# K and V in rows of 64 KiB, V blocks in turn in one overlapping buffer

One core of one Trainium2 chip. The metric is the device time of one execution in microseconds (us), median of several executions. Profiled spans are some 2 us shorter than the timed executions.

## The reference, cut to what matters

One decode step of an attention layer over a long cache, times a small gated dense branch:

```python
q = xn @ wq                                   # 1 x (16 heads x 256)
scores = einsum("bhqd,bhkd->bhqk", q, k_cache) * 256 ** -0.5   # 65536 keys per head
o = einsum("bhqk,bhkd->bhqd", softmax(scores), v_cache)
s = o.reshape(1, 1, 4096) @ wo
out = x + s * silu(silu(xn @ w1) @ w2)        # xn = layernorm(x), x: 1 x 1 x 448
```

K and V are 16 x 65536 x 256 bf16 each, 1074 MB together, and each byte is used once. The weights are 10.6 MB.

## The kernel before

A block is 128 partitions x 128 keys (4 blocks per head, 64 in all). Each block of K, and of V, comes as two tiles of 64 keys, 32 KiB per partition, each into its own buffer. VectorE multiplies K by the query (19 of 32 keys with a fused multiply and sum, 13 as one product that ScalarE then sums), ScalarE makes the exponentials, TensorE multiplies them with V, two keys per matmul. Scores of block i run beside V of block i - 1.

```python
KT, SUB, ND, TPB = 64, 32, 19, 2
Kt = [pool.tile([P, KT * Dh], bf16, name=f"K{t}") for t in range(TPB)]
Vt = [pool.tile([P, KT * Dh], bf16, name=f"V{t}") for t in range(TPB)]

def sp_block(i):                      # the only issuer of the stream
    for t in range(TPB):
        take(sp, kf[t])               # K buffer t is free
        sp.dma_start(out=Kt[t][:, :], in_=src(Kd, i, t)).then_inc(kl[t], 16)
        take(sp, vf[t])               # V buffer t is free
        sp.dma_start(out=Vt[t][:, :], in_=src(Vd, i - 1, t)).then_inc(vl[t], 16)

def pe_attend():
    take(pe, pv)                      # exponentials of the block
    for t in range(TPB):
        take(pe, vl[t], 16)           # V tile t has landed
        pe_keys(psO, Vt[t], 0, t * KT, KT, t == 0, t == TPB - 1, ...)   # 32 matmuls, then the buffer is free
# ... query copied per block from a broadcast table; products go to separate buffers prod[], junk_d[], junk_a[]
# ... start (layernorm, q, dense branch), last block and output projection left out
```

## Time and profile before

| | before |
|---|---|
| median, range of 4 | 2529.24 us, 2528.04 to 2529.59 |
| DMA, mid-run | 16 engines busy, 432 GB/s |
| one block (16 MiB of K and V), mid-run | 38.87 us |
| VectorE, TensorE, ScalarE busy | 88%, 51%, 57% |
| last packet of the stream, end | 2519.7, 2527.2 us |

A DMA of 128 rows is spread over 16 DMA engines, 8 rows each, one packet per row here. The engines do not march together: one ends its share up to 4 us before another. "Landing" below is the end of the slowest engine's share; a block's period is the time from one landing of V to the next; a burst is the run of matmuls that multiplies one block's exponentials with V; the release is the moment in a burst after which the next V may be issued, and its lead is the time from that issue to the moment when the first engine has done its share of the K queued before it. Packet times are from the trace's records of single packets, put on the same clock as the instructions; they do not name the engine, so what is said of single engines is put together from the times. The lines themselves are in the prediction.

### The profile page before, as it was taken

The numbers are of one execution on the slowest core, as the hardware profiler recorded it, in microseconds if no ns is written. First come the engines' busy times: TensorE is split into PE (matmuls) and PEld (weight loads), VectorE is DVE, ScalarE is ACT, GpSimd is POOL, SyncE is SP. The second block draws the span as 40 slices with busy tenths as digits, with TensorE's granted clock in tenths as the row PEclk, the third lists the DMA queues.
The fourth block names the chain that finished last, engine by engine and source line by source line (L and its number), as shares of the span: only waits on it lengthen the run. The fifth ranks groups of instructions, "written<-read, shape, count | busy, mean of one in ns | idle before, by whom it ended". The sixth has DMA issues, their size and how long they took to land. (4 is left out here: it accounts for less than half of the span.)

```text
span 2527.2 us, 30558 instructions
## 1 busy us (share of the span) xinstructions
PE 1284.5 (51%) x4945; PEld 483.4 (19%) x4945; DVE 2219.2 (88%) x10276; ACT 1446.6 (57%) x6996; POOL 1.4 (0%) x12
## 2 busy tenths in 40 slices
PE   3554455455544554555455445544554455445547
PEld 1111121111111211111112111111121111111212
DVE  7989898898898988988989889889898898898886
ACT  5656565655565656555656565556565655565553
POOL 0000000000000000000000000000000000000000
PEclk7777777777777777777767776777677767776778
DMA  9999999999999999999999999999999999999998
GB/s 413 432 432 432 432 432 432 432 432 432 432 432 433 432 433 432 432 432 432 432 432 432 432 432 432 432 432 432 432 432 432 432 432 433 432 432 432 432 432 346
DMA packets 40450, 1084.46 MB, mean 429 GB/s; under 512 B 4338, under 2 KB 6516, under 8 KB 6644
## 3 DMA queue, kind: packets, MB, share of 16 engines
q1 hardware_dynamic: 40434, 1084.31, 99.8%
q8 instruction: 4, 0.07, 0.0%
q14 instruction: 10, 0.08, 0.0%
q10 hardware_dynamic: 2, 0.00, 0.0%
HBM read 1084.29 MB, written 0.00 MB: 429 GB/s over the span
## 5 line engine op out<-in xcount | busy, mean ns | idle before, releaser
L262 ACT ACTIVATE junk_a<-prod 128x256 bf16<-128x256 bf16 x3328 | 1330.7, 401 | 746.9 <-ACTq L141 746.9
L308 PE MATMUL psO<-V,PV 128*2 128x512 bf16 x4064 | 1165.2, 458 | 1097.6 <-PEq L141 1097.6
L226 DVE CUSTOM_DVE_ANT_0 junk_d<-K,qcur 128x256 bf16<-128x256 bf16 x4864 | 1698.7, 414 | 0.0
L308 PEld LDWEIGHTS psO<-V,PV 128*2 128x2 bf16 x4064 | 388.4, 97 | 1847.6 <-issue 1520.3
L212 DVE TENSOR_TENSOR prod<-K,qcur 128x3328 bf16<-128x3328 bf16 x256 | 482.9, 1886 | 247.0 <-DVEq L141 247.0
L262 ACT ACTIVATION_READ_ACCUMULATOR junk_a<-prod 128x1 f32 x3328 | 620.0, 186 | 0.0
L226 DVE DVE_READ_ACCUMULATOR2_ANT S<- 128x1 f32 x4864 | 374.2, 77 | 0.0
L295 ACT COPY O<-psO 2x512 f32<-2x512 f32 x64 | 36.8, 574 | 202.4 <-ACTq L141 202.4
L343 PE MATMUL ps_t<-eye,O 2*128 2x1 f32 x520 | 69.6, 251 | 48.4 <-PEq L141 48.4
L343 PEld LDWEIGHTS ps_t<-eye,O 2*128 2x128 f32 x520 | 65.9, 192 | 69.0 <-issue 68.9
L297 ACT COPY hist<-ps_t 128x2 f32 (+1 forms) x65 | 10.4, 160 | 94.9 <-ACTq L141 94.9
L301 PE MATMUL ps_nb<-gmax,ones_row 1*128 1x1 bf16 x65 | 10.3, 159 | 56.1 <-PEq L141 55.6
L191 DVE COPY qcur<-qb 128x256 bf16 (+1 forms) x64 | 14.5, 227 | 25.4 <-issue 15.8
L284 ACT ACTIVATE PV<-S,hist 128x128 bf16<-128x128 f32 (+1 forms) x65 | 26.0, 400 | 2.1
L199 DVE COPY S<-S 128x128 f32<-128x128 f32 (+1 forms) x65 | 14.7, 226 | 9.5
L200 DVE TENSOR_REDUCE rmax<-S 128x1 bf16<-128x128 f32 (+1 forms) x65 | 18.2, 280 | 0.2 <-issue 0.2
L180 DVE TENSOR_REDUCE gmax<-ps_m 1x1 bf16<-1x128 f32 x65 | 17.8, 274 | 0.5 <-DVEq L141 0.5
L301 PEld LDWEIGHTS ps_nb<-gmax,ones_row 1*128 1x128 bf16 x65 | 6.0, 92 | 60.8 <-issue 60.5
L333 PE MATMUL ps_m<-ident,rmax 128*1 128x128 bf16 x65 | 14.3, 220 | 5.7 <-PEq L141 5.7
L488 PE MATMUL ps_a<-xnT,V 128*64 128x1 bf16 x112 | 6.7, 256 | 18.2 <-DMA V<-in_B_w_dram 18.2
L284 ACT ACTIVATION_READ_ACCUMULATOR PV<-S,hist (+1 forms) x65 | 12.1, 186 | 0.0
L488 PEld LDWEIGHTS ps_a<-xnT,V 128*64 128x64 bf16 x112 | 6.6, 210 | 18.7 <-DMA V<-in_B_w_dram 18.7
(65 smaller groups left out, 79.3 us busy)
## 6 DMA issues: line engine op xcount, KB each, us to landing
K<-in_A_k_cache_dram SPq DMA_DIRECT2D x126, 4096.0 KB, 21.3
V<-in_A_v_cache_dram SPq DMA_DIRECT2D x125, 4096.0 KB, 28.7
K<-in_A_k_cache_dram SPq DMA_DIRECT2D x4, 2048.0 KB, 18.5
V<-in_A_v_cache_dram SPq DMA_DIRECT2D x4, 2048.0 KB, 22.9
W<-in_A_v_cache_dram SPq DMA_DIRECT2D x2, 2048.0 KB, 27.3
W<-in_A_wq_dram SPq DMA_DIRECT2D x1, 3072.0 KB, 10.4
K<-in_A_wo_dram SPq DMA_DIRECT2D x3, 896.0 KB, 31.4
V<-in_B_w_dram SPq DMA_DIRECT2D x1, 1568.0 KB, 35.5
```

Source lines behind the costliest of these rows:

```text
L180: dve.reduce_max(out=gmax[0:1, :], in_=ps_m[0:1, :], axis=AX.X).then_inc(gm, 1)
L191: q_t = own(dve.tensor_copy(out=qcur[:, :], in_=qb[:, sub(q0, Dh)]))
L199: dve.tensor_copy(out=S2[:, c0:c1], in_=S[:, c0:c1]).then_inc(f, 1)
L200: dve.reduce_max(out=rmax[:, :], in_=S[:, c0:c1], axis=AX.X).then_inc(rm, 1)
L212: m = dve.tensor_tensor(out=prod[k % 2][:, :, :], in0=Kv[:, s * SUB + ND : (s + 1) * SUB, :], in1=qcur[:, None, :].to_broadcast([P, NA, Dh ...
L226: ins = dve.tensor_tensor_reduce(out=junk_d[jk][:, :], in0=Kv[:, s * SUB + j, :], in1=qcur[:, :], scale=1.0, scalar=0.0, op0=ALU.mult, op1 ...
L262: ins = act.activation(out=junk_a[jk][:, :], in_=prod[k % 2][:, j, :], func=ACT.Identity, accum_out=S[:, a : a + 1],)
L284: act.activation(out=PV[:, c0:c1], in_=S2[:, c0:c1], func=ACT.Exp, bias=neg, scale=scale, accum_out=hist[:, at(i), 1:2].rearrange("p o s - ...
L295: act.copy(out=O[:, :], in_=po[:, :]).then_inc(oc, 1)
L301: pe.matmul(ps_nb[:, 0:1], lhsT=ones_row[0:1, :], rhs=gmax[0:1, :], start=True, stop=True).then_inc(bm, 1)
L308: ins = pe.matmul(po[:, :], lhsT=PV[:, c0 + c : c0 + c + 2], rhs=T[:, (k0 + c) * Dh : (k0 + c + 2) * Dh], start=(start and c == 0), stop=( ...
L343: ins = pe.matmul(ps_t[:, a : a + 1], lhsT=Ov[:, j, a, :], rhs=eye2[:, j : j + 1], start=(j == 0), stop=(j == 1),)
```

## The change

Its intent: halve the number of packets, and so their fixed cost, by loading whole blocks in 64 KiB rows. K keeps two buffers, now of 64 KiB per partition; V gets, in place of two, one buffer of 140 keys (70 KiB), in which odd blocks begin 12 keys further on than even ones. The 116 keys that the next block will overwrite are multiplied first; then its load is issued. The product buffers go (products are written over K), and so does the broadcast query table. The core of the diff:

```diff
-KT = 64
+KB = 128
+VO = 12
-    Kt = [pool.tile([P, KT * Dh], bf16, name=f"K{t}") for t in range(TPB)]
-    Vt = [pool.tile([P, KT * Dh], bf16, name=f"V{t}") for t in range(TPB)]
-    prod = [...]; junk_d = [...]; junk_a = [...]; qb = ...
+    Kt = [pool.tile([P, KW], bf16, name=f"K{t}") for t in range(2)]
+    Vb = pool.tile([P, KW + VO * Dh], bf16, name="V")
+    Vt = [Vb[:, t * VO * Dh : t * VO * Dh + KW] for t in range(2)]
+    def load_k(i, s):
+        take(sp, kf[s])
+        sp.dma_start(out=Kt[s][:, :], in_=block(Kd, i)).then_inc(kl[s], 16)
+    def load_v(i, t):
+        take(sp, vf)
+        sp.dma_start(out=Vt[t], in_=block(Vd, i)).then_inc(vl, 16)
+    # stream: K0 K1 | V0 K2 | V1 K3 | ...
+    def pe_block(i, t):
+        first = (VO, KB) if t == 0 else (0, KB - VO)      # 116 keys, 58 matmuls
+        rest = (0, VO) if t == 0 else (KB - VO, KB)       # 12 keys, 6 matmuls
+        take(pe, pv)
+        take(pe, vl, 16)
+        pe_keys(psO, Vt[t], *first, True, False, vf)      # then the next V may be issued
+        pe_keys(psO, Vt[t], *rest, False, True, od)
+        pe_rows(); pe_query(i + 1); pe_bcast(); pe_turn()
```

The last K comes in halves, the last two V in parts of 8 to 32 keys among the parts of wo; the order of the end is new. The start loads all weights before K0.

## The prediction

> **What bounds the kernel now.** I read the page first: the engines' shares, the DMA lines in 40 slices, and the packet count.
>
> ```profile
> span 2527.2 us, 30558 instructions
> PE 1284.5 (51%) x4945; PEld 483.4 (19%) x4945; DVE 2219.2 (88%) x10276; ACT 1446.6 (57%) x6996; POOL 1.4 (0%) x12
> ...
> DMA  9999999999999999999999999999999999999998
> GB/s 413 432 432 432 432 432 432 432 432 432 432 432 433 432 433 432 432 432 432 432 432 432 432 432 432 432 432 432 432 432 432 432 432 433 432 432 432 432 432 346
> DMA packets 40450, 1084.46 MB, mean 429 GB/s; under 512 B 4338, under 2 KB 6516, under 8 KB 6644
> ```
>
> VectorE is busiest among the engines (88%), but all 16 DMA engines are busy in every slice, and the rate stays at 432 GB/s in 38 of 40 slices: the kernel streams 1074 MB of K and V once, and the stream is the bound. The chain of waits names only the last 30 us and says nothing of this. Next, whether the queue ever runs dry, from the list of DMA issues (size, median us from issue to landing):
>
> ```profile
> K<-in_A_k_cache_dram SPq DMA_DIRECT2D x126, 4096.0 KB, 21.3
> V<-in_A_v_cache_dram SPq DMA_DIRECT2D x125, 4096.0 KB, 28.7
> ```
>
> A 4 MiB tile takes 9.72 us of stream time (mid-run completions follow each other at 1187.77, 1197.48, 1207.20, 1216.91 us), and it lands 21 to 29 us after its issue: it waits behind one or two others, so a next transfer is always queued. The packet records agree: in mid-run never fewer than 16 packets are in flight.
>
> So the time per packet decides. From the records of single packets (start, duration, bytes), median or shortest duration: 4 KiB 159 ns, 10.5 KiB 404, 16 KiB 611, 24 KiB 912, 32 KiB 1213 (32,128 of these, mean 1217). These lie on one line: bytes / 27.2 GB/s + 8.8 ns. For 32 KiB that is 1204.7 + 8.8 = 1213.5. A completion adds one 4-byte packet of 9 ns per engine. Check: 8 packets per engine and tile, 8 x 1213.5 + 9 = 9717 ns, the 9.72 us above.
>
> **What the Trainium skill says.** "DMA: Bandwidth & Descriptors", section "Where 436 GB/s comes from", gives 16 ports x 32 B x 850 MHz = 435.2 GB/s, or 27.2 per engine: the slope of my line. Only 0.7% (432 against 435.2) is left above it. Its section "Why small descriptors are slow (HBM only)" has a fixed cost of about 3 cycles per packet; this trace shows 8.8 ns, 7 to 8 cycles at 850 MHz, so the measured size is used. Its section "Latency and other measured facts" warns that HBM row pitches at large powers of two can lose rate (512 KiB pitch 207 GB/s, 4 MiB 103); pitch doubles here from 32 to 64 KiB, and no run yet shows whether this matters. "TensorE: Matmul & The Clock Gate", Part 1, says that TensorE starts at half clock after an idle window of about 3.4 us and doubles after one busy window. The trace agrees, in the weight loads of one burst (0.43 us apart, then 21 in 4.40 us, 0.21 apart) and in the bursts themselves:
>
> ```profile
> 1211.16 0.13 PEld L308 LDWEIGHTS psO<-V,PV 128*2 128x2 bf16 x1 [0.30 <-issue]
> 1211.58 0.13 PEld L308 LDWEIGHTS psO<-V,PV 128*2 128x2 bf16 x1 [0.30 <-issue]
> 1211.99 4.40 PEld L308 LDWEIGHTS psO<-V,PV 128*2 128x2 bf16 x21 [0.28 <-issue]
> ```
>
> ```profile
> 1188.36 8.59 PE L308 MATMUL psO<-V,PV 128*2 128x512 bf16 x32 [7.33 <-PEq L141]
> 1207.79 9.11 PE L308 MATMUL psO<-V,PV 128*2 128x512 bf16 x32 [10.84 <-PEq L141]
> 1227.23 9.62 PE L308 MATMUL psO<-V,PV 128*2 128x512 bf16 x32 [7.34 <-PEq L141]
> ```
>
> **The change, part by part.** *Rows of 64 KiB.* A block of 128 keys was two tiles for K and two for V; now it is one transfer each, 128 packets of 64 KiB instead of 256 of 32 KiB. If a row is one packet, it takes by the line 2409.4 + 8.8 = 2418.2 ns; 8 of them and one completion are 19,355 ns per 8 MiB, against 2 x 9717 = 19,434. Saved: 79 ns. Whole-block loads are 63 of K and 62 of V, 125 x 79 ns = 9.9 us. The end is cut finer: before, 20 MiB came in 16 KiB rows (80 packets per engine for 40 of 32 KiB); after, 14 MiB come in 16 KiB, 1 MiB in 8 KiB and 1 MiB in 4 KiB rows (80 packets for 32), 8 more extra packets x 8.8 ns = 0.1 us back. Sum: -9.8 us.
>
> *V in turn in one buffer.* V of the next block overlaps 116 of the present block's 128 keys, so its load waits until 58 of 64 matmuls are done, where before each half had its own buffer. Put V's landing at 0 (slowest engine). PE starts 0.6 us later (landing 1207.20, burst 1207.76 to 1207.79). 58 matmuls at 0.2135 us are 12.4 us; from bursts of 8.35 to 10.02 us for 32, 8 to 15 of them run at half clock, adding 1.6 to 3.2: 14.0 to 15.6. Last matmul to SP's issue 0.25 us (burst end 1196.95, issue 1197.20); issue to first packet about 0.9 us (first load: 0.96 to 1.9). So the next V is ready 15.7 to 17.3 us after the landing. Meanwhile the queue holds K, 19.35 us. The slowest engine keeps 2 to 3.6 us of reserve. The fastest engine runs 2.8 to 4 us ahead (spread of one transfer's completions, early and late in the run), so it will run dry for up to 2 us; as every engine carries the same bytes, the slowest sets the end, and this costs nothing but the spread. Cost: 0, but with little room.
>
> *Products in place in K, and VectorE's load.* The rows:
>
> ```profile
> L226 DVE CUSTOM_DVE_ANT_0 junk_d<-K,qcur 128x256 bf16<-128x256 bf16 x4864 | 1698.7, 414 | 0.0
> ...
> L212 DVE TENSOR_TENSOR prod<-K,qcur 128x3328 bf16<-128x3328 bf16 x256 | 482.9, 1886 | 247.0 <-DVEq L141 247.0
> ```
>
> Per block 4 x 1.886 + 76 x 0.345 (start to start) = 33.8 us, unchanged. The maximum over partitions, which used to hide behind the next product, is now waited for at the block's end: two small reductions, the copies and the trip to PE, an estimated 2.2 us from these instructions' durations (0.23, 0.28, 0.22, 0.27) and 0.15 to 0.3 us per hand-over. So about 36 us per block against a stream of 38.7: VectorE stays inside, with 2 to 3 us to spare. K comes free at the block's end some 20 us before its reload is due. The query is now broadcast by PE per block (one 256-column matmul): beside other work.
>
> *Start.* The first bytes are the same; K0 and K1 now follow all weights. VectorE starts at about 39.6 instead of 15 us, frees K0 at about 73.6, and K2 is due at 77.6 us of stream: ready in time by some 2.8 us. VectorE then lags by a block, and catches up over some dozen blocks.
>
> *End.* Before, the last packet of wo lands at 2519.7 and the span ends at 2527.2: 7.5 us, of which the last two VectorE operations and the output's 2.7 us are a floor. After: the last V parts land, by the line, about 3.8 us before the last of wo (6 heads of 1792-byte rows, 48 packets x 78 ns per engine); after them come 8 matmuls, the copy, the turn, the last head's projection and the same two operations and store. Adding their durations from the timeline I get 7 to 8.5 us after the last packet. Change: 0 to +1 us, called 0.
>
> Sum: 2529.0 - 9.8 = 2519.2 us, -0.4%.
>
> **Rivals.** (1) The hardware cuts a 64 KiB row in two: no packet is saved, only 125 completions x 9 ns; about 2528. For it: no 64 KiB packet exists in this trace. Against: nothing seen. (2) V is released too late. If the burst started cold throughout, 58 x 0.427 = 24.8 us, each of some 62 loads would be 7 us late, +400 us; the bursts above show that it warms up. A release 1 us beyond the reserve would cost 62 us, 2590. (3) VectorE becomes the bound: a block over 38.7 us instead of 36; each us above costs 64 us. TENSOR_TENSOR writing where it reads would have to slow by 0.7 us each. (4) Larger pitch disturbs HBM: packets show now almost no contention (mean 1217 for 1213), and the rate needed is unchanged; 1% slower packets would make 2544. (5) The end loses 2 to 3 us to the longer chain after the last part of V: 2522.
>
> **Range and chances.** The sum has one large, well-determined term; the one-sided risks are stalls. I take 2519 with 2514 to 2528 for 8 in 10. Faster by over 2% would need 2478 us, below 1084.3 MB / 435.2 GB/s = 2491.5 us of pure transfer: excluded in practice, 0.01. Slower by over 2% (2580) needs a stall in every block: 0.04. Within 2%: 0.95.
>
> **What would show it.** Right: packets of 64 KiB, about 16,000, near 2418 ns; packet total near 22,600 (16,000 + 256 + 896 + 128 + 256 data packets for 33,412 of 16 and 32 KiB, and some 2000 completions fewer); 433 to 434 GB/s in mid-run; still 16 packets in flight, or a completion spread that shrinks below 3 us; V about 23 us and K about 41 us from issue to landing; PE bursts of 16 to 17 us once per block; VectorE's idle time mostly at K's landing. Wrong: 32 KiB packets still there; slices under 430 GB/s; gaps between K's last packet and V's first; VectorE without any wait for K.

## The result

The changed kernel takes 2539.31 us (median of 4, 2537.19 to 2541.05) against 2529.24: ratio 1.004, 95% interval 1.0023 to 1.0058. Ratios here are the mean time of one kernel's fast runs over that of the other's of the same rounds, so not quite the ratio of the medians. The forecast was -9.8 us; it became +10.1. That the change stays within 2% came true; its sign did not, and 2539 lies outside the range of 2514 to 2528.

The page of the kernel after (share of the span; GB/s in 40 equal slices; packets):

```profile
span 2539.3 us, 29819 instructions
PE 1164.2 (46%) x5051; PEld 472.9 (19%) x5051; DVE 2231.8 (88%) x10281; ACT 1449.3 (57%) x6990; POOL 2.5 (0%) x13
...
GB/s 419 428 432 431 433 433 436 432 433 424 427 424 427 429 438 432 418 429 429 429 430 440 435 429 429 430 429 427 430 427 430 431 428 429 423 422 428 440 425 334
DMA packets 22582, 1084.48 MB, mean 427 GB/s; under 512 B 2338, under 2 KB 4516, under 8 KB 4900
```

The packets are fewer, as wanted: 16,000 of 64 KiB, each one packet, with a median of 2418 ns, the forecast to the nanosecond. But the rate, which was 432 in nearly every slice, now drops to 422 to 430 in many. The mean 64 KiB packet took 2437.5 ns, 19.5 above the median; at 1000 such packets per engine that is 19.5 us. So the loss sits in a minority of slow packets, and the question is which.

The list of DMA issues (median us from issue to landing) says that V is queued with little to spare:

```profile
K<-in_A_k_cache_dram SPq DMA_DIRECT2D x63, 42.7
V<-in_A_v_cache_dram SPq DMA_DIRECT2D x62, 23.9
```

A whole block takes 19.35 us to stream, so K waits 23 us in the queue, V only 4.6 until the slowest engine is done with K. I sorted the 64 KiB packets by the time since the latest V issue. Of the 15,500 or so in the stream's middle, 359 that took more than 200 ns too long began within 5 us after an issue of V, and some 27 in the other 34 us of the period. Slow packets are V's first and second packets (and K's last beside them).

Two blocks from the timeline of TensorE, a good one and a bad one (start us, duration us, instruction, count, idle before). V landed at 1211.54 and at 1755.09:

```profile
1212.02 15.59 PE L316 MATMUL bank<-V,PV 128*2 128x512 bf16 x64 [20.82 <-PEq L156]
...
1755.56 16.87 PE L316 MATMUL bank<-V,PV 128*2 128x512 bf16 x64 [21.19 <-PEq L156]
```

And the issue that follows the second burst, from the timeline of the DMA queue's issuer:

```profile
1771.38 0.33 SPq L197 DMA_DIRECT2D V<-in_A_v_cache_dram  x1
```

The burst was 1.3 us longer because more of it ran at half clock (14 matmuls 0.43 us apart before the spacing falls to 0.216, against 8), so V was issued 16.29 us after the landing, not 15.02. The first DMA engine ran out of K 1.04 us after that issue. In this block 26 packets of V took over 200 ns too long, and V took 21.22 us instead of 19.32. In the good block the issue came 2.67 us ahead of the first engine, and V took 19.32.

What the packets look like when V is really late (issue at 1150.11, 0.09 us after the first engine had finished K; start us, duration ns, bytes):

```
1150.015     9       4     <- an engine's completion of K: it has nothing to do now
1150.029     9       4
1151.065  3105   65536     <- V's first packet on an engine that had run dry: 0.96 us after the issue
1151.069  3200   65536
1151.318  3453   65536
1154.166  2420   65536     <- V's second packet: normal again
```

An engine that has run dry loses the gap and then 0.6 to 1.0 us in its first packet.

But an engine need not run dry to be slowed. In the bad block above 13 of the 16 engines went from K to V without a gap, and the first ten of these took 2.66 to 3.29 us for their first packet; the other three paused for at least 0.4 us, though V had been issued 1.7 us or more before, and took 3.28 to 3.85. Over the whole stream, 847 first packets of V followed the last of K within 20 ns, and 203 of them took more than 200 ns too long; 113 came after a gap, and 86 of these did. Among the 847 the time since V's issue sorts them: of 104 that began 0.9 to 1.6 us after it 95 were slow, of 235 that began 3 us or more after it 17.

The other lines that were to stay did: VectorE's two costly rows are the same to 3 ns on average, although they now write where they read.

```profile
L249 DVE CUSTOM_DVE_ANT_0 K<-K,qcur 128x256 bf16<-128x256 bf16 x4864 | 1700.3, 417 | 0.3 <-issue 0.3
...
L238 DVE TENSOR_TENSOR K<-K,qcur 128x3328 bf16<-128x3328 bf16 x256 | 482.7, 1885 | 130.6 <-DVEq L156 130.4
...
L214 DVE TENSOR_REDUCE gmax<-bank 1x1 bf16<-1x128 f32 x65 | 18.3, 281 | 108.4 <-DVEq L156 108.4
```

(The idle time of the third is the trip to TensorE at the block's end, 108.4 / 65 = 1.7 us per block.) VectorE needs 35.5 us per block while it lags (K is issued at 74.64, 110.13, 145.92 us), inside the stream's 38.7.

The end became longer. The chain that ended last, in order of time, before:

```profile
2512.46 3.54 PE ps_a L308 x16
2516.00 1.51 PE ps_ao L679 x8
2517.52 1.03 PE ps_t L343 x8
2518.55 4.64 PE ps_ao L679 x24
```

and after:

```profile
2495.57 26.25 DMA V<-in_A_v_cache_dram
...
2521.86 5.30 PE bank L316 x16
2527.16 1.03 PE bank L344 x8
2528.19 3.54 PE bank L316 x16
2531.74 1.51 PE bank L639 x8
2533.25 1.03 PE bank L344 x8
2534.28 0.96 PE bank L639 x4
```

After the landing of keys 64 to 95 of the last V, TensorE is busy without a pause to the end, and its first 16 matmuls take 5.30 us because the clock is down for most of the first twelve (the first three are 0.215 us apart, the next nine 0.30 to 0.43, the others 0.216). From the last packet to the end it is 9.5 us (2529.8 to 2539.3), 2.0 more than before.

### The profile page after: what moved, and what is told of

It reads as the page before. It is cut to its first block, busy times and chain, and to the rows that moved or that the text cites. A ratio compares the mean times of both kernels' runs of the same rounds, so it can differ in the third digit from the quotient of the medians.

```text
span 2539.3 us, 29819 instructions
## 1 busy us (share of the span) xinstructions
PE 1164.2 (46%) x5051; PEld 472.9 (19%) x5051; DVE 2231.8 (88%) x10281; ACT 1449.3 (57%) x6990; POOL 2.5 (0%) x13
## 5 line engine op out<-in xcount | busy, mean ns | idle before, releaser
L271 ACT ACTIVATE K<-K 128x256 bf16<-128x256 bf16 x3328 | 1330.7, 401 | 709.3 <-ACTq L156 709.2
L249 DVE CUSTOM_DVE_ANT_0 K<-K,qcur 128x256 bf16<-128x256 bf16 x4864 | 1700.3, 417 | 0.3 <-issue 0.3
L316 PE MATMUL bank<-V,PV 128*2 128x512 bf16 x4032 | 1016.8, 419 | 1244.5 <-PEq L156 1239.5
L316 PEld LDWEIGHTS bank<-V,PV 128*2 128x2 bf16 x4032 | 361.6, 90 | 1872.1 <-issue 1440.6
L271 ACT ACTIVATION_READ_ACCUMULATOR K<-K 128x1 f32 x3328 | 620.1, 186 | 5.1 <-issue 5.1
L238 DVE TENSOR_TENSOR K<-K,qcur 128x3328 bf16<-128x3328 bf16 x256 | 482.7, 1885 | 130.6 <-DVEq L156 130.4
L297 ACT COPY O<-bank 2x512 f32<-2x512 f32 x66 | 37.8, 573 | 199.2 <-ACTq L156 199.2
L214 DVE TENSOR_REDUCE gmax<-bank 1x1 bf16<-1x128 f32 x65 | 18.3, 281 | 108.4 <-DVEq L156 108.4
L344 PE MATMUL bank<-eye,O 2*128 2x1 f32 x528 | 74.5, 258 | 2.7
L305 ACT COPY hist<-bank 128x2 f32 (+1 forms) x65 | 10.4, 160 | 112.5 <-ACTq L156 112.4
L344 PEld LDWEIGHTS bank<-eye,O 2*128 2x128 f32 x528 | 70.7, 201 | 8.1 <-issue 1.3
L231 DVE CAST qcur<-bank 128x256 bf16<-128x256 f32 x64 | 27.2, 425 | 16.2 <-DVEq L156 16.0
L224 DVE COPY S<-S 128x128 f32<-128x128 f32 (+1 forms) x65 | 14.7, 226 | 9.5
## 6 DMA issues: line engine op xcount, KB each, us to landing
K<-in_A_v_cache_dram SPq DMA_DIRECT2D x4, 2048.0 KB, 17.3
V<-in_A_wq_dram SPq DMA_DIRECT2D x1, 3072.0 KB, 10.4
V<-in_A_v_cache_dram SPq DMA_DIRECT2D x1, 1024.0 KB, 16.2
```

Of the source, the lines that this page charges most:

```text
L214: dve.reduce_max(out=gmax[0:1, :], in_=ps_m[0:1, :], axis=AX.X).then_inc(gm, 1)
L224: dve.tensor_copy(out=S2[:, c0:c1], in_=S[:, c0:c1]).then_inc(kf[s], 1)
L231: dve.tensor_copy(out=qcur[:, :], in_=ps_q).then_inc(sd, 1)
L238: m = dve.tensor_tensor(out=pair, in0=pair, in1=qcur[:, None, :].to_broadcast([P, NA, Dh]), op=ALU.mult,)
L249: ins = dve.tensor_tensor_reduce(out=Kv[:, c, :], in0=Kv[:, c, :], in1=qcur[:, :], scale=1.0, scalar=0.0, op0=ALU.mult, op1=ALU.add, accum ...
L271: ins = act.activation(out=prod, in_=prod, func=ACT.Identity, accum_out=S[:, c : c + 1],)
```

## The experiments

The theory after the result, L: V is released too late. The issue comes when the first DMA engines are within a microsecond or two of the end of K; they run dry or nearly so, and the packets that follow are slow. Rivals: R, rows of 64 KiB are slow now and then by themselves; S, loading V into a buffer that TensorE is still reading costs the transfer. Twelve kernels ran, all with correct results, and all in the fast state except the one of experiment 5, a single execution whose state is unknown. The kernel before had a median of 2529.3 to 2529.6 beside each group.

**1. Early release.** V in two transfers of 64 keys; the first may overwrite keys that are multiplied first, so it is issued after 26 to 32 matmuls.

```diff
-        take(sp, vf)
-        sp.dma_start(out=Vt[t], in_=block(Vd, i)).then_inc(vl, 16)
+        for k0, k1, f in ((0, 64, va), (64, KB, vf)):
+            take(sp, f)
+            load_keys(Vt[t], block(Vd, i), k0, k1, vl)
...
-        take(pe, vl, 16)
-        pe_keys(psO, Vt[t], *first, True, False, vf)
+        take(pe, vl, 32)
+        mid = VO + 64 if t == 0 else 64 - VO
+        pe_keys(psO, Vt[t], first[0], mid, True, False, va)
+        pe_keys(psO, Vt[t], mid, first[1], False, False, vf)
```

> The changed kernel with each V block loaded as two transfers of 64 keys (32 KiB rows); the first is issued after 26 to 32 of the 64 matmuls, the second as now after 58. Theory L (V is released too late: its first packets find the engines of the DMA run dry or about to): every V is queued 7 us or more before K ends, so the 22 us by which the 60 block periods exceed 38.64 us go away; 8 more packets per engine and block x 8.8 ns x 62 = 4.4 us come back: about 2521 to 2523 us, period 38.7. Rival R (64 KiB rows are themselves slow now and then): the slow packets of V go away because V has 32 KiB rows, those of K stay; about 2530. Rival S (writing V into a buffer that PE is reading costs the transfer): nothing changes but the 4 us: 2543.

Measured: 2527.34 us (2526.96 to 2529.1), ratio to before 0.9994 (0.9981 to 1.0006). The slow packets are gone from V and from K: 64 KiB packets, still used for K, have a mean of 2422.3 ns, the 32 KiB ones 1217.1 as in the kernel before. V's first part is issued 5 us and more ahead of the first engine. The period is 38.78 us. L's own figure (2521 to 2523) was missed by some 4 us: 0.08 us above the 38.7 hoped for are 5 us in 61 blocks. By its time alone the run lies between L and R (2530); what speaks for L is that R's slow packets in K are not there.

**2. The same packets, late release.** Both parts wait for the 58th matmul.

```diff
+        take(sp, va)
+        take(sp, vf)
+        for k0, k1 in ((0, 64), (64, KB)):
+            load_keys(Vt[t], block(Vd, i), k0, k1, vl)
```

> The same two transfers per V block, but both issued only after 58 matmuls. Only the time of release differs from split_early. Theory L: the stalls stay, 2538 to 2546 us, V periods up to 40 us where the issue is less than some 1.6 us ahead of K's first engine. Rival R: as split_early, within 3 us of it.

Measured: 2552.76 us (2548.41 to 2556.91), ratio 1.009. 25.4 us lie between two kernels that move the same rows in the same packets into the same overlapping buffer and differ in when V is issued. In the mid-run (430 to 2400 us) 591 of the 32 KiB packets and 45 of the 64 KiB ones took over 200 ns too long, in experiment 1 none of either. This decides against R and S. It is worse than L's range for it; why a late V in two transfers is worse than in one was not followed up.

**3. The dose, first form.** Blocks 4 and 8 keys apart instead of 12: 62 and 60 matmuls before the release.

```diff
-VO = 12
+VO = 4        (and 8)
```

> The changed kernel with V blocks 4 keys apart instead of 12: PE must finish 62 matmuls instead of 58 before the next V is issued, 0.85 us later. Theory L: the issue moves to 15.6 to 17.3 us after V's landing, nearly all blocks have less than 1.6 us of lead and lose about 1 us each as the late ones do now: 2555 to 2580 us. Rivals R and S (size of row, shared buffer) predict 2539 as now.

> Blocks 8 keys apart: 60 matmuls before the release, 0.43 us later than now and 0.43 us earlier than vo4. Theory L: between the changed kernel (2539) and vo4 (2550.5): 2542 to 2548. Rivals: 2539.

Measured: 2550.53 us (2547.33 to 2555.91) for 4 and 2545.27 (2543.3 to 2552.87) for 8. With 12: 2539.3. The mean period goes 39.01, 39.11, 39.21 us. For 4 keys I had expected more (2555 to 2580): the engines' spread narrows where V is late, so the dose is blunted. The direction and order are L's; R and S have none.

**4. The clock, not the buffer.** TensorE multiplies nothing of use between bursts, only to keep its clock up, so that the 58 matmuls need 12.4 us. Order, buffers and rows are untouched.

```diff
         pe_bcast()
         pe_turn()
+        for _ in range(82):
+            pe.matmul(bank[7][0:2, :], lhsT=ident[:, 0:2],
+                      rhs=ident[:, 0:1].to_broadcast([P, 2 * Dh]), start=True, stop=True)
```

> The changed kernel with 82 idle matmuls on TensorE after each block from block 23 on, so that its clock is still up when V lands; buffers, rows and order are untouched. Theory L: 58 matmuls take 12.4 us instead of 14 to 15.6, V is issued about 13.2 us after its landing, and the 15.5 us of excess in the blocks from 23 on go away, those of 6.9 us before them stay: about 2524 us. Rivals R and S: 2539.

Measured: 2544.06 us, from 2533.83 to 2553.53: a miss, and an unsteady one. The timeline of TensorE shows why (idle before in brackets):

```profile
1416.62 15.46 PE L316 MATMUL bank<-V,PV 128*2 128x512 bf16 x64 [3.60 <-PEq L156]
1433.92 18.02 PE L381 MATMUL bank<-ident 128*2 128x512 bf16 x82
1455.48 13.97 PE L316 MATMUL bank<-V,PV 128*2 128x512 bf16 x64 [3.55 <-PEq L156]
```

82 were too few. Before the 39 bursts that followed idle matmuls TensorE stood idle for 3.0 to 4.6 us. 8 of these bursts (after 3.4 to 3.8 us) took 13.97 us, all at full clock; the other 31, after idle times both shorter and longer, began at half clock. The Trainium skill, "TensorE: Matmul & The Clock Gate", Part 1, has the clock go down after an idle window of about 3.4 us, in windows that run freely. The trace agrees roughly: near that length the clock was down before most bursts and up before others, down already after 3.0 us of idleness. The release mostly stayed at 14.7 to 16.5 us. The few blocks that were released at 13.4 to 13.5 us mostly had periods of 38.64 to 38.70. With 92 idle matmuls, from block 9 on:

> As warm, with 92 idle matmuls in place of 82 and from block 9 on. In warm TensorE stood idle for 3.55 to 3.60 us before many bursts, and these bursts took 15.5 us (clock down again), the others 14.0. 10 more matmuls leave some 1.5 to 2 us idle. Theory L: nearly all bursts at 14 us, V issued 13.2 us after its landing, 3.5 us or more ahead of the first engine; periods of 38.64 to 38.75; 2518 to 2522 us, under the kernel before. Rivals (row size, shared buffer, or a busier TensorE taking something from the transfers): 2535 to 2545 as in warm.

```profile
1436.96 13.97 PE L316 MATMUL bank<-V,PV 128*2 128x512 bf16 x64 [1.61 <-PEq L156]
```

Now V is issued 13.5 us after its landing, 4.1 us ahead of the first engine, block after block (three blocks: 15.0 and 2.7 us, and no loss), and the periods are 38.70 us for 50 blocks in a row, without a slow packet. The stream's mid-run, one window per kernel (us, busy time of each engine, granted clock, DMA share, GB/s), before:

```profile
430.00:2400.00 1970.00, 997.87 (x3767) 371.94 (x3768) 1749.89 (x8118) 1139.76 (x5533) 0.00 (x0) 0.72 1.00 432
```

after the change:

```profile
430.00:2400.00 1970.00, 899.78 (x3823) 358.15 (x3821) 1747.89 (x8071) 1137.87 (x5495) 0.00 (x0) 0.70 1.00 430
```

and with the clock kept up:

```profile
430.00:2400.00 1970.00, 1876.54 (x8498) 736.66 (x8498) 1765.69 (x8148) 1150.20 (x5555) 0.00 (x0) 0.97 1.00 433
```

The idle matmuls alone turn 430 into 433, and the last data packet of the stream ends at 2513.1 us, against 2529.8 after the change and 2519.7 before. The DMA share reads 1.00 in all three: a slow packet counts as busy, so this column cannot show the loss. The whole run, though, took 2534.22 us (2531.11 to 2537.29), not 2518 to 2522: the idle matmuls also ran after the last block and held up the end (16.2 us from the last data packet to the end; the 12.2 and the "last packet at 2517" of a later expectation count a packet of fetched instructions as the last), and the first eight blocks kept their stalls.

**5. The dose, second form.** With the clock kept up, 0, 6, 10 or 14 idle matmuls ahead of the release, in four stretches of 12 blocks in one execution.

```diff
-        pe_keys(psO, Vt[t], *first, True, False, vf)
+        pe_keys(psO, Vt[t], *first, True, False, None if hold else vf)
+        # hold - 1 idle matmuls, then one that does then_inc(vf, 1)
```

> A dose in one trace: TensorE's clock is kept up as in warm92, so that the release comes at a fixed time, and 0, 6, 10 and 14 idle matmuls of 0.21 us stand before the release in four stretches of 12 blocks (blocks 9, 21, 33, 45). V is then issued about 13.5, 14.8, 15.7 and 16.5 us after its landing, and the first engine of the DMA runs out of K some 4.2, 2.9, 2.1 and 1.2 us after the issue. Theory L: periods of 38.70, about 38.7, 38.9 and 39.4 us (from the changed kernel's blocks sorted by this lead: over 2.4 us 38.73, 1.6 to 2.4 us 38.89, less 39.37). Otherwise (busy TensorE, order) all four alike.

Measured, one profile (2557 us in all), first block of each stretch left out, since the switch from one loop to the next delays it:

| idle matmuls ahead of the release | 0 | 6 | 10 | 14 |
|---|---|---|---|---|
| V issued after its landing, median us | 13.49 | 14.79 | 15.59 | 18.13 |
| mean period, us | 38.76 | 38.89 | 39.03 | 40.02 |

The last stretch lost its rhythm (some releases at 18 and 19 us) and is beyond what was meant; with 6 and 10, too, the releases are not fixed but fall on two values (14.8 and 16.4 us; 15.6 and 17.3). All four periods are above the forecast. The order is L's, and it comes with TensorE kept as busy in all four, so that its being busy is not what helps; the threshold can be read from single blocks: in the changed kernel, periods by the time from V's issue to the moment when the first engine ends K were 38.69 us for 2.4 to 3.2 us (12 blocks), 38.90 for 1.6 to 2.4 (29), 39.62 for 0.8 to 1.6 (14). One block with more than 3.2 us took 39.21; there not V was late but the K before it. Below 0.8 (5 blocks) the period was 38.74: there the engines that run dry are those that were far ahead, and the slowest is spared. In the other kernels with late release such blocks did lose (39.36 and 39.55 with 8 and 4 keys), so this is not a rule.

**6. What the rows are worth.** As experiment 1, but K in 32 KiB rows too.

```diff
-        sp.dma_start(out=Kt[s][:, :], in_=block(Kd, i)).then_inc(kl[s], 16)
+        for k0, k1 in ((0, HK), (HK, KB)):
+            load_keys(Kt[s], block(Kd, i), k0, k1, kl[s])
```

> split_early with K too in two transfers of 64 keys, so that all rows of whole blocks have 32 KiB as before the change; release early. It measures what the longer rows are worth: by my prediction's line 63 x 79 ns = 5.0 us over split_early (2532), by the periods without a stall (38.64 against 38.87 us for 16 MiB, 117 ns per 8 MiB) 7.4 us (2535). If rows are worth nothing: 2527.

Measured: 2532.83 us (2531.76 to 2534.48), 5.5 over experiment 1: 87 ns per 8 MiB block of K, near the 79 of the prediction's line. So the expected gain of the rows is real. With late release and short rows only:

> split_late with K in 32 KiB rows too: late release and only short rows. Theory P (an engine of the DMA must find its next descriptor when it starts its last packet, so a 64 KiB packet needs 2.4 us of lead and a 32 KiB one 1.2): most of the 25 us between split_late and split_early go away, 2535 to 2542 us. Theory Q (the lead needed does not hang on the packet's length): the stalls stay and 7 us for the rows come on top, 2555 to 2562.

Measured: 2550.37 us (2542.07 to 2556.3). 17.5 us over split_k32: some two thirds of the 25.4 us that late release costs with 64 KiB rows of K. Neither P nor Q fits cleanly, and the four runs spread over 14 us; that late release costs much with short rows as well is the part that stands.

**7. Better versions.** Three tries to keep the rows' gain without the stalls.

> Candidate to beat both: idle matmuls in blocks 7 to 60 only (warm92 had them after the last block too, where they held up the end: 12.2 us from the last packet to the end against 9.5), and the turn of the first half of the last block moved into a pause of TensorE (1.0 us). From warm92's stream (last packet at 2517 in its profile) and a tail of 8.5 us: 2524 to 2528.

Measured: 2526.43 us (2525.67 to 2529.88), ratio 0.9991 (0.9977 to 1.0004). Most blocks have 38.70 us, but the switch out of the loop cost one block dear (timeline of TensorE; V had landed at 2404.62):

```profile
2383.41 21.86 PE L381 MATMUL bank<-ident 128*2 128x512 bf16 x92
...
2409.15 16.64 PE L316 MATMUL bank<-V,PV 128*2 128x512 bf16 x64 [3.87 <-PEq L156]
```

In this pause TensorE's sequencer stands at the loop's branch until 2408.74, and a 16 KiB packet of the kind "instruction" is fetched (2406.26, 1.07 us). Such packets stand at each switch of the loops that were added, and nowhere in the mid-run of the changed kernel.

> split_early with the same move of the turn at the end. At the end TensorE is busy without a pause from the landing of keys 64 to 95 of the last V (2509.8) to 2521.5; one turn of 1.03 us less in it: 1.0 us off, 2526.3. If the end hangs on the last packet instead: no change, 2527.3.

Measured: 2527.07 us (2526.12 to 2527.52), ratio 0.9991: 0.3 us below experiment 1, within the scatter. The moved turn waited for ScalarE's copy and ran at 2509.6, just ahead of the same unbroken run of matmuls, so it did not use the pause. A miss.

> The changed kernel with 88 idle matmuls ahead of each block's wait for V, from block 7 to the last (not after it), and the moved turn. In warm_best the switch out of the loop with idle matmuls came after them: TensorE then stood still for 3.9 us past its last idle matmul, V was released 19.97 us after its landing instead of 13.5, and that V took 22.9 us instead of 19.35. With the idle matmuls first in a block the switch falls into idle time: 3 us off warm_best, 2522 to 2524, clearly under the kernel before (2529.3). If idle matmuls on TensorE cost the transfers something by themselves: 2526 or more.

Measured: 2528.47 us (2526.95 to 2530.16), ratio 0.9997. A miss: the late blocks are now at 38.70 us, but the switch into the loop, ahead of its first 88 idle matmuls, delays block 7 instead (release 19.66 us after the landing), and blocks 2 to 6, which have no idle matmuls, lost up to 1.6 us each. No version was faster than the kernel before by more than the interval allows.

## Why the prediction was wrong

The step that failed is in "V in turn in one buffer": "it will run dry for up to 2 us; as every engine carries the same bytes, the slowest sets the end, and this costs nothing but the spread. Cost: 0, but with little room."

The sizes that lead up to this sentence were right. V was to be issued some 14.85 to 16.45 us after its landing (the step's sum without the last 0.9); it was 14.69 to 16.44. The burst was to be 16 to 17 us; the two shown took 15.59 and 16.87. The slowest engine was to have some 2 to 4 us; it had 2.9 to 5.0 from the issue. The rows gained what they should: the period without stalls is 38.70 us against 38.87.

Wrong was that an engine short of descriptors loses only its lead. The first packet of one that ran dry takes 3.0 to 3.5 us instead of 2.42; one that goes over to V without a gap is slow as well if V was issued less than some 1.6 us before (95 of 104); where V arrives just as many engines end K, packets of engines that come later are slow too, up to 3.8 us; and so the slowest engine is hit in the end, although V was there some 3 us ahead of it. The bad block shows it whole: 16.29 us to the issue, 3.03 us ahead of the slowest engine, and V 1.9 us too long. The reserve has to be counted from the first engine, and in these runs it had to be over some 2.4 us.

The sum, with what was measured in place of what was forecast:

| term | forecast | measured |
|---|---|---|
| rows: period without stalls, 61 blocks of 16 MiB | -9.8 us in all | (38.70 - 38.87) x 61 = -10.4 |
| late V: mean period above that | 0 | (39.01 - 38.70) x 61 = +18.9 |
| end, last packet to end | 0 (0 to +1) | +2.0 |
| sum | -9.8 | +10.5 |

The profiled runs differ by 12.1 us, the medians by 10.1; 1.6 us of the profiled difference are in none of the terms (start and the finer cuts at the end were not tried by themselves). That the late V causes the second term is shown by experiments 2 and 4: the same packets issued earlier, or the same kernel with a faster burst, and it goes. Rival 2 of the prediction had the right cause with the wrong threshold: it let a release cost only when it passed the slowest engine's reserve. (Its figure for 1 us beyond the reserve, 2590, does not follow from its own sum: 2519 + 62 = 2581.)

Of the other steps: VectorE stayed inside the stream (35.5 us per block while lagging, forecast 36; it caught up in 7 blocks, not a dozen). The end was undersized: 7 to 8.5 us forecast, 9.5 measured, 1.7 of it from 16 matmuls of which most ran at a clock that had gone down (5.30 against 3.61 us in experiment 1, where the end takes 7.9 us, inside the forecast). Two of the signs named as "wrong", slices under 430 GB/s and gaps between K's last packet and V's first, came.

What stays open is by what a late V slows packets, on engines that never ran dry above all. The traces show that it does, and that the time since its issue matters, but not the mechanism.

## What to carry to other kernels

A stream that is bound by DMA needs its next transfer queued well before the first of the 16 engines is done, not just before the last is: here about 2.4 us before. Larger transfers save fixed cost per packet, but if a buffer's reuse then puts compute between one landing and the next issue, the reserve must be worked out for the slowest form of that compute, here a burst that starts at half clock. If the gain is 0.4%, a stall of 0.3 us per block of 38.7 us (0.8%) takes it twice over.

## What the Trainium skill lacked or had wrong

- "DMA: Bandwidth & Descriptors" gives no figure for how far ahead a transfer must be queued, or for a DMA engine that has run dry. Here: first packets of 3.0 to 3.5 us instead of 2.42 after running dry, 95 of 104 first packets slow that began 0.9 to 1.6 us after the issue, periods 0.9 us longer at a lead of 0.8 to 1.6 us, nearly none over 2.4 us.
- The same page, "Why small descriptors are slow (HBM only)", has about 3 cycles of fixed cost per packet, and 32 bytes of descriptor metadata per DMA operation beside it; the packets here, 4 to 64 KiB, fit 8.8 ns, 7 to 8 cycles of its 850 MHz. It states no time for a 64 KiB row: one packet, 2418 ns.
- Its figures on row pitch ("Latency and other measured facts") begin at 512 KiB. Here, at 64 KiB, no loss showed: the median packet took 2418 ns, on the line of the shorter rows.
- No page that I read gives the length of the pause at a switch from one loop to the next. "Runtime: NRT & Kernel Launch", section "Instruction fetch mechanics", names a stall for fetching instructions at a taken branch, without a figure; here TensorE stood still for 3.87 us in experiment 7, with a fetch of 16 KiB in the pause.
